# Alpha's signs made later, and other filler products at the start, in a banded attention with a PReLU feed-forward

## The chip, the cores and the metric

One core of a Trainium2 chip runs the program. TensorE (PE; PEld is its weight load) multiplies, VectorE (DVE), ScalarE (ACT) and GpSimd (POOL) do the elementwise work, and DMA queues on SyncE (SP) and ScalarE move data. The metric is the device time of one execution in microseconds: the median of 3 runs of the kernel before is 830.37 us (830.01 to 830.52).

## The reference

Attention in a causal window of 64 positions over 8 batches of 576 positions and 8 heads of 64, and behind it a feed-forward layer with a leaky rectifier whose slope alpha differs by hidden unit:

```python
scores = scale * np.matmul(q, k.transpose(0, 1, 3, 2))
mask = (rel >= 0) & (rel < window)
scores = np.where(mask, scores, -1000000000.0)
...
x = attn_out.transpose(0, 2, 1, 3).reshape(4608, 512)
h = x @ w_in                                       # 512 -> 2048
g = np.maximum(h, 0.0) + alpha * np.minimum(h, 0.0)
out = g @ w_out                                    # 2048 -> 512
```

The weights arrive as 64-bit floats and are taken apart on the chip into a high and a low 32-bit part.

## The kernel before

The 4608 tokens are 36 tiles of 128, in nine groups of four. For a tile, TensorE makes scores (`score`, L594), VectorE masks them and takes the row's maximum (L636), ScalarE takes the exponential (L642), VectorE the reciprocal of its sum (`recip`, L668 and L669), GpSimd scales (`scale`, L673), TensorE turns the result over (`turn`, L690), ScalarE or VectorE copies it from PSUM (`put`, L695 and L697), TensorE multiplies with the values (`value`, L733), and two more steps split that into a high and a low part (`x_high` L742, `x_low` L745). A hidden block of 128 units and its share of the output make a cell: `hidden` (L1204), the rectifier (L840, L847), its two parts (L853, L857), and the output products (L874). In the first 100 us the same engines also convert the 32 weight blocks (`weights`): `expo` (L436, L438), `shift` (L443, L446), `tail` (L451), `join` (L455), `total` (L459) and the two parts (L474, L478).

The rectifier needs, per hidden unit, the sign of 1 - alpha and alpha times that sign (`s_sb`, `sa_sb`); the sign bit (`flip_sb`) is also put into each block of `w_out` by its `shift`. `signs` makes all three from alpha, which was loaded, and turned by TensorE into a PSUM bank (`alpha_t`).

Every piece is a step with planned engine times; a planner puts the steps in order with a table of due times (`DUE`, `BEGIN`), and each engine's queue is written out in that order and worked off strictly in turn. Behind the plan, `fill` looks at TensorE's planned gaps up to 28 us and fills them with products that nobody reads (`plan.idle`, L391): a 128x128 block of zeros times itself, in 32-bit floats, into a spare PSUM bank. A product in 32-bit floats runs as two passes on the chip, each with its weight load. At the far end `quarter` (L1167, L1165, L1171) sums and stores the last four quarters of the output; a wanted time sets their order.

Of the kernel before, what the change touches and what calls it, by code (L numbers as in the profile page):

```python
# [18 lines left out]
PE, DVE, ACT, POOL, SP = "PE", "DVE", "ACT", "POOL", "SP"  # L19
# [6 lines left out]
WARM = 28.0  # L26
# [105 lines left out]
class Plan:  # L132
# [5 lines left out]
    def step(self, engines, emit, after=(), behind=(), take=(), give=(), want=math.inf, moved=0.0, span=0.0,  # L138
             port=False):

        s = Step(engines, emit, after, list(behind), list(take), list(give), want, moved, span, port)
        for a in s.after + s.behind:
            a.before.append(s)
        s.group = self.group
        self.steps.append(s)
        return s
# [110 lines left out]
    def fill(self, done):  # L260

        some, t = [], 1.3
        for s in sorted((s for s in done if s.engine == PE), key=lambda s: s.start):
            while t + 0.4 < min(s.start, WARM):
                hold = 0.22 if t > 6.0 else 0.3
                some.append(Step({PE: (hold, hold)}, self.idle, (), (), (), (), math.inf, 0.0, 0.0, False))
                some[-1].start, some[-1].end, some[-1].engine = t, t + hold, PE
                t += hold
            t = max(t, s.start + s.engines[PE][0])
        return some  # L270
# [28 lines left out]
def banded_attention_then_prelu_ffn(  # L299
# [11 lines left out]
    nc = tc.nc  # L311
    P = 128
    D = 64
    W = WINDOW
# [40 lines left out]
    sa_sb = const.tile([P, NF], F32, name="sa_sb")  # L355
# [30 lines left out]
    plan = Plan(stock)  # L386
    plan.stock["o"].append((WARM + 1.0, 3))
    spare = ps.tile([P, P], F32, tag="b3", name="spare")
    nought = xs_of["l", 1][:, 0, (NBLK - 1) * P:].bitcast(F32)
    nc.vector.memset(nought, 0.0)  # L390
    plan.idle = lambda _: nc.tensor.matmul(spare, nought, nought, start=True, stop=True)  # L391
    step = plan.step

    def turned_in(x):
# [14 lines left out]
    def room(b, shape, dtype, name):  # L409
        return sb.tile(shape, dtype, tag=str(b.at), name=name)  # L410
# [5 lines left out]
    def weights(c):  # L416
        plan.group = "w", c, 0
        f, odd = divmod(c, 2)
        d = cv[c]
        last = 2 * NF - 1 - c  # L420
        raw = Buffer("raw", 2, [None, "new", "v", "kk"][max(0, 3 - last)])
        val, low = (Buffer(kind, 1, "os" if last < 2 else None) for kind in ("val", "low"))
        two = Buffer("o" if c < 4 else "bank", 1)

        def fetch(_):
            t = room(raw, [P, 2 * E] if odd else [P, NP, 2 * P], I32, f"raw_{c}")
            nc.sync.dma_start(t, w_out[f * P:(f + 1) * P, :] if odd else
                              w_in[:, 2 * f * P:2 * (f + 1) * P].rearrange("(c p) f -> p c f", p=P))
            t = t if odd else t.rearrange("p a b -> p (a b)")
            t = t.rearrange("p (n t) -> p n t", t=2)  # L430
            d["low"], d["high"] = t[:, :, 0].bitcast(U32), t[:, :, 1]

        def expo(e):
            d["two"] = t = bank(two, [P, E], I32, f"two_{c}")
            if e == ACT:
                nc.scalar.activation(t.bitcast(F32), d["high"].bitcast(F32), AF.Copy, scale=2.0**-112)  # L436
            else:
                nc.vector.tensor_scalar(out=t.bitcast(F32), in0=d["high"].bitcast(F32), scalar1=2.0**-112,  # L438
                                        scalar2=None, op0=ALU.mult)

        def shift(_):
            if odd:
                nc.vector.tensor_scalar(out=d["two"], in0=d["two"], scalar1=3, scalar2=flip_sb[:, f:f + 1],  # L443
                                        op0=ALU.logical_shift_left, op1=ALU.bitwise_xor)
            else:
                nc.vector.tensor_scalar(out=d["two"], in0=d["two"], scalar1=3, scalar2=None,  # L446
                                        op0=ALU.logical_shift_left)

        def tail(_):
            d["tail"] = room(low, [P, E], I32, f"low_{c}")  # L450
            nc.scalar.activation(d["tail"], d["low"], AF.Copy, scale=2.0**-29)  # L451

        def join(_):
            d["val"] = room(val, [P, E], I32, f"val_{c}")
            nc.vector.scalar_tensor_tensor(out=d["val"], in0=d["high"], scalar=-2**31, in1=d["two"],  # L455
                                           op0=ALU.bitwise_and, op1=ALU.bitwise_xor)

        def total(_):
            nc.gpsimd.tensor_tensor(out=d["val"], in0=d["val"], in1=d["tail"], op=ALU.add)  # L459

        name = "wout" if odd else "win"

        def late(part):
            return [Buffer("late " + z, 1) for n, f0, z in LATE if (n, f0) == (name + part, f)]

        def begin(part):
            for n, f0, z in LATE:
                if (n, f0) == (name + part, f):
                    f1 = min([x for m, x, _ in LATE if m == n and x > f0], default=NF)
                    parts_of[n][f0] = sb.tile([P, f1 - f0, E], F32R, tag=z, name=f"{n}_{f0}")  # L470

        def high(_):
            begin("_h")
            nc.scalar.copy(weight(name + "_h", f), d["val"].bitcast(F32))  # L474

        def rest(e):
            begin("_l")
            (nc.gpsimd if e == POOL else nc.vector).tensor_tensor(  # L478
                out=weight(name + "_l", f), in0=d["val"].bitcast(F32), in1=weight(name + "_h", f).bitcast(F32),
                op=ALU.subtract)  # L480

        s0 = step({SP: (0.4, 0.4)}, fetch, take=[raw], moved=1.5 if odd else 1.65, span=1.75 if odd else 2.3)
        s1 = step({ACT: (0.55, 0.63), DVE: (0.6, 0.69)}, expo, [s0], take=[two])
        s2 = step({DVE: (0.66, 0.75) if odd else (0.6, 0.69)}, shift, [s1] + [alphas] * odd)
        s3 = step({ACT: (0.56, 0.66)}, tail, [s0], take=[low], give=[raw])
        s4 = step({DVE: (0.6, 0.68)}, join, [s2], take=[val], give=[raw, two])
        s5 = step({POOL: (1.22, 1.28)}, total, [s3, s4], give=[low])
        prior = cv[c - 2]["done"] if c >= 2 else [None, None]
        s6 = step({ACT: (0.51, 0.61)}, high, [s5], prior[:1] if prior[0] else [], take=late("_h"))
        s7 = step({POOL: (1.22, 1.28), DVE: (0.59, 0.68)}, rest, [s6], prior[1:] if prior[0] else [],  # L490
                  take=late("_l"), give=[val], port=True)
        d["done"] = [s6, s7]
# [340 lines left out]
    def behind(ts, f, d, done, hb, want_o, cols, coarse=True):  # L833
# [2 lines left out]
        gb, ghb, glb = Buffer("g", 1), Buffer("gh", 1), Buffer("gl", 1)  # L836

        def slopes(_):
            d["g"] = room(gb, [P, NBLK * P], F32, f"g_{ts[0]}_{f}")[:, :nt]
            nc.scalar.activation(d["g"], d["h"][:, :nt], AF.Copy, scale=sa_sb[:, f:f + 1])  # L840


        start = ts[0] < NBLK
# [33 lines left out]
        hold = {2: (1.46, 0.37, 0.40, 0.31, 0.69), 4: (2.72, 0.57, 0.667, 0.53, 1.24)}[n]  # L877
        lat = {2: (1.55, 0.475, 0.485, 0.405, 0.74), 4: (2.87, 0.69, 0.75, 0.62, 1.28)}[n]
        if f == 0:
            for t in ts:  # L880
# [5 lines left out]
                  give=[hb if start else gb])  # L886
# [3 lines left out]
        for todo in todos:  # L890
# [5 lines left out]
                      give=[ghb] + [glb] * lows, want=want_o)  # L896
# [5 lines left out]
        if f == NF - 1:  # L902
# [3 lines left out]
            for i, t in enumerate(ts):  # L906
                for x in parts(t):
                    sbuf, os = Buffer("g" if t == NT - 1 else "gh" if t == NT - 2 else "os", 1), {}
# [11 lines left out]
                    def store(e, t=t, x=x, os=os):  # L920
# [6 lines left out]
                             give=[ob[t]], want=want_o + 3 + i)  # L927
                    step({ACT: (0.4, 0.4)} if x.start else {SP: (0.4, 0.4)}, store, [c],
                         give=old if apart else [sbuf], moved=0.8 / m)
# [4 lines left out]
    entries_o, kept_o, slots, acc, mid = {}, {}, {}, {}, {}  # L934
# [49 lines left out]
    def behind_last(ts, f, d, done, hb, want_o, cols):  # L984
# [5 lines left out]
        lh, rh = slice(0, 2 * P), slice(2 * P, 4 * P)  # L990
# [127 lines left out]
        a1 = step(half, lambda _: vec(slots[i][:, rh], slots[i][:, rh], d["g"][:, rh], ALU.add), [s2], port=True)  # L1118
# [63 lines left out]

        last, u4_of = lambda: acc["P1"], lambda: u["u4"]
        quarter("os", 1, lh, lambda: acc["P7"], lambda: u["u2"], [p4, u2, u4], want_o + 3.0)
        quarter("os", 1, rh, u4_of, lambda: mid["P7"], [u4], want_o + 3.2)
        quarter("gh", 0, rh, lambda: acc["P3"], lambda: u["u4"], [p3, u4], want_o + 3.5)
        quarter("gl", 0, lh, last, None, [p2], want_o + 4.0)

# [228 lines left out]
    al, ab = {}, Buffer("o", 1)  # L1417
# [2 lines left out]
        al["t"] = bank(ab, [P, NF], F32, "alpha_t")  # L1420
        nc.tensor.transpose(al["t"], alpha_sb, ident[:NF, :NF])

    def signs(_):
        a = al["t"]
        nc.vector.tensor_scalar(out=s_sb, in0=a, scalar1=1.0, scalar2=-2.0, op0=ALU.is_gt, op1=ALU.mult)
        nc.vector.tensor_scalar_add(s_sb, s_sb, 1.0)
        nc.vector.tensor_scalar(out=flip_sb, in0=s_sb.bitcast(I32), scalar1=-2**31, scalar2=None, op0=ALU.bitwise_and)
        nc.vector.tensor_tensor(out=sa_sb, in0=s_sb, in1=a, op=ALU.mult)

    a0 = step({ACT: (0.64, 0.64)}, load_alpha, moved=0.1)  # L1430
    a1 = step({PE: (0.2, 0.4)}, turn_alpha, [a0], take=[ab])
    alphas = step({DVE: (0.8, 0.8)}, signs, [a1], give=[ab], want=20.0)

    plan.group = "z", 0, 0
    new = Buffer("new", 1, "pt")
# [123 lines left out]
```

## Time and profile before

| | us |
|---|---|
| median of 3 runs | 830.37 |
| the profiled execution | 831.18 |
| its span, from the first to the last instruction | 829.3 |
| PE busy in it | 819.8 (99%) |
| DVE busy | 596.6 (72%) |
| ACT busy | 486.3 (59%) |
| POOL busy | 426.2 (51%) |

The busy share of PE counts the filler products too, and is an average over a start in which other engines set the pace and a long stretch in which PE does. The granted clock is 1.00 over the span.

### The profile page before, as it was taken

What the parts mean: (1) busy time and instruction counts of PE and PEld (TensorE: products, weight loads), DVE (VectorE), ACT (ScalarE), POOL (GpSimd) and SP (SyncE); (2) the same over time, 40 slices, a digit from 0 to 9 for tenths busy, and PEclk for the clock granted to TensorE, in tenths of its full rate; (3) what the DMA queues carried; (4) which work ended last, traced back from release to release, by engine and by line L of the source; (5) the groups of instructions that cost most, each with busy time, mean ns of one, the idle gap of its engine ahead of it and who ended that gap; (6) DMA issues with size and microseconds to landing.
All of it is one profiled execution on the core that took longest, in us unless ns stands there. A gap on an engine that the chain in (4) does not pass through costs nothing.

```text
span 829.3 us, 21484 instructions
## 1 busy us (share of the span) xinstructions
PE 819.8 (99%) x7943; PEld 748.3 (90%) x7943; DVE 596.6 (72%) x1675; ACT 486.3 (59%) x1297; POOL 426.2 (51%) x424
## 2 busy tenths in 40 slices
PE   9999999999999999999999999999999999999997
PEld 8888888888999999999999999999999999998997
DVE  6999979997666573888496678658787639525665
ACT  6999986567464634655454646465646446434542
POOL 4888776896433333646365435544454533222462
PEclk9999999999999999999999999999999999999999
DMA  9587756484766566776677675768676765467765
GB/s 312 188 269 212 211 183 202 171 264 142 241 180 202 154 183 211 230 197 193 225 193 240 191 252 153 247 183 244 197 242 180 217 202 150 109 215 224 242 219 165
DMA packets 128679, 170.75 MB, mean 206 GB/s; under 512 B 9776, under 2 KB 82496, under 8 KB 128576
## 3 DMA queue, kind: packets, MB, share of 16 engines
q1 hardware_dynamic: 127408, 168.34, 66.8%
q8 instruction: 63, 1.03, 0.5%
q10 hardware_dynamic: 1168, 1.06, 0.4%
q14 instruction: 40, 0.33, 0.1%
HBM read 141.04 MB, written 28.31 MB: 204 GB/s over the span
## 4 chain that ended last, share of the span: by engine, by line
PE 92%; ACT 3%; DVE 2%; DMA 1%; POOL 1%; issue 1%; SPq 0%; DVEq 0%; ACTq 0%; POOLq 0%
PE o L874 38%; PE h L1336 31%; PE h L1204 8%; PE acc_P L1045 4%; PE av L733 4%; PE s L612 3%; PE s L594 1%; PE spare L391 1%; DMA win_h<-kept 1%; PE t L690 1%; DVE val L455 1%; ACT low L451 0%; POOL val L459 0%; ACT two L436 0%; DMA out<-os 0%
## 5 line engine op out<-in xcount | busy, mean ns | idle before, releaser
L857 POOL TENSOR_TENSOR gl<-g,gh 128x512 fp32r<-128x512 f32 x112 | 144.3, 1296 | 207.5 <-ACT gh L853 121.3
L874 PE MATMUL o<-wout_h,gh 128*128 128x512 f32 x512 | 196.9, 385 | 0.0
L874 PE MATMUL o<-wout_l,gh 128*128 128x512 f32 x512 | 194.2, 379 | 0.0
L840 ACT ACTIVATE g<-h,sa_sb 128x512 f32<-128x512 f32 (+1 forms) x132 | 89.2, 676 | 127.8 <-DVE h L1363 113.9
L874 PE MATMUL o<-wout_h,gl 128*128 128x512 f32 x512 | 136.0, 379 | 0.0
L713 DVE STREAM_TRANSPOSE pt<-w 32x256 f32<-32x256 f32 x312 | 128.5, 426 | 4.7
L847 DVE SCALAR_TENSOR_TENSOR g<-h,s_sb,g 128x512 f32<-128x512 f32 x112 | 83.9, 749 | 33.9 <-ACT g L840 32.4
L874 PEld LDWEIGHTS o<-wout_h,gh 128*128 128x128 f32 x512 | 97.1, 190 | 12.2 <-issue 0.5
L874 PEld LDWEIGHTS o<-wout_h,gl 128*128 128x128 f32 x512 | 95.8, 189 | 13.2 <-POOL gl L857 0.2
L874 PEld LDWEIGHTS o<-wout_l,gh 128*128 128x128 f32 x512 | 97.2, 190 | 9.6 <-DVE wout_l L478 0.3
L853 ACT CAST gh<-g 128x512 fp32r<-128x512 f32 x112 | 69.3, 620 | 49.4 <-DVE g L847 48.4
L1363 DVE TENSOR_TENSOR h<-h,w 128x256 f32<-128x256 f32 x56 | 24.2, 433 | 100.2 <-PE h L1336 98.3
L652 ACT ACTIVATE w<-w,nm 128x96 f32<-128x96 f32 x208 | 76.1, 373 | 13.4 <-DVE nm L646 13.3
L673 POOL TENSOR_TENSOR w<-w,rc 128x768 f32<-128x768 f32 (+2 forms) x44 | 59.0, 1341 | 46.3 <-DVE rc L669 35.6
L1373 ACT COPY u<-h 128x256 f32<-128x256 f32 x112 | 41.7, 373 | 53.8 <-PE h L1336 53.6
L1336 PE MATMUL h<-xh,win_l 128*128 128x256 f32 x336 | 64.9, 275 | 0.0
L1336 PE MATMUL h<-xh,win_h 128*128 128x256 f32 x336 | 63.5, 277 | 0.0
L1336 PEld LDWEIGHTS h<-xh,win_h 128*128 128x128 f32 x336 | 55.0, 190 | 6.9 <-DVE h L1363 0.3
L1336 PE MATMUL h<-win_h,win_l 128*128 128x256 f32 x336 | 59.8, 281 | 0.0
L1363 DVE TENSOR_TENSOR h<-h,u 128x256 f32<-128x256 f32 x112 | 47.5, 427 | 12.4 <-PE h L1336 8.0
L1336 PEld LDWEIGHTS h<-xh,win_l 128*128 128x128 f32 x336 | 51.8, 192 | 0.5
L1336 PEld LDWEIGHTS h<-win_h,win_l 128*128 128x128 f32 x336 | 50.0, 191 | 0.9
(205 smaller groups left out, 1855.2 us busy)
## 6 DMA issues: line engine op xcount, KB each, us to landing
win_h<-kept SPq DMA_DIRECT2D x112, 256.0 KB, 2.8
win_l<-kept SPq DMA_DIRECT2D x112, 256.0 KB, 3.0
v<-vN SPq DMA_DIRECT2D x72, 256.0 KB, 4.6
stream<-kept SPq DMA_DIRECT2D x56, 256.0 KB, 2.9
k<-kT SPq DMA_DIRECT2D x35, 384.0 KB, 4.1
q<-qT SPq DMA_DIRECT2D x34, 256.0 KB, 4.4
raw<-w_in SPq DMA_DIRECT2D x16, 512.0 KB, 4.3
raw<-w_out SPq DMA_DIRECT2D x16, 512.0 KB, 4.1
```

Source lines behind the costliest of these rows:

```text
L652: nc.scalar.activation(w, w, AF.Exp, scale=-1.0, bias=d["nm"][:, g:g + 1], accum_out=d["sm"][:, g:g + 1])
L673: nc.gpsimd.tensor_tensor(out=w, in0=w, in1=d["rc"][:, g].unsqueeze(2).broadcast_to(list(w.shape)), op=ALU.mult)
L713: nc.vector.transpose(dst[:, :, i * SUB:(i + 1) * SUB], d["w"][r, :, :, k * SUB:(k + 1) * SUB].rearrange("p e h k -> p (e h) k"))
L840: nc.scalar.activation(d["g"], d["h"][:, :nt], AF.Copy, scale=sa_sb[:, f:f + 1])
L847: nc.vector.scalar_tensor_tensor(out=g, in0=d["h"][:, :nt], scalar=s_sb[:, f:f + 1], in1=d["g"], op0=ALU.mult, op1=ALU.max)
L853: nc.scalar.copy(d["gh"], d["g"])
L857: (nc.vector if start else nc.gpsimd).tensor_tensor(out=d["gl"], in0=d["g"], in1=d["gh"].bitcast(F32), op=ALU.subtract)
L874: nc.tensor.matmul(po[t], gt[:, cols[i] * P:(cols[i] + 1) * P], turned_in(weight(wt, f)), start=(f == 0 and k == 0), stop=(f == NF - 1 and ...
L1204: nc.tensor.matmul(ph[:, :nt], weight(wt, f)[:, c * P:(c + 1) * P], turned_in(tokens_of(xt, xs)[:, c]), start=(k == 0), stop=(k == 3 * NP ...
L1336: nc.tensor.matmul(out, a[:, c * P:(c + 1) * P], turned_in(b[c]), start=start and i == c == 0, stop=i == 2 and c == 1, skip_group_check=True)
L1363: nc.vector.tensor_tensor(out=out, in0=a, in1=b, op=ALU.add)
L1373: nc.scalar.copy(d["u"][i], d[x])
```

## The change

The time at which alpha's signs are made moves: the step that ran `signs` behind alpha's turn now only copies alpha from PSUM to `sa_sb` (`take_alpha`), and the four instructions of `signs`, now reading that copy, are sent from inside the first `shift` of a `w_out` block. `fill` has other bounds: before 11 us of planned time it leaves gaps of up to 0.3 us open, from there to 24 us up to 1.1 us, then 0.5 us (it was 0.4 us throughout); and up to 6 us it puts in pairs of products with 48 moving columns (`plan.cold`) with a planned 0.4 us a pair, in place of one of 128 with 0.3 us. One wanted time at the end is 0.5 us later.

```diff
-            while t + 0.4 < min(s.start, WARM):
-                hold = 0.22 if t > 6.0 else 0.3
-                some.append(Step({PE: (hold, hold)}, self.idle, (), (), (), (), math.inf, 0.0, 0.0, False))
+            while t + (0.3 if t < 11.0 else 1.1 if t < 24.0 else 0.5) < min(s.start, WARM):
+                hold = 0.22 if t > 6.0 else 0.4
+                some.append(Step({PE: (hold, hold)}, self.idle if t > 6.0 else self.cold, (), (), (), (), math.inf, 0.0, 0.0, False))
...
+    def cold(_):
+        for _ in range(2):
+            nc.tensor.matmul(spare[:, :W * 3 // 4], nought, nought[:, :W * 3 // 4], start=True, stop=True)
...
         def shift(_):
+            if odd and not al.get("done"):
+                al["done"] = True
+                signs()
             if odd:
...
-        quarter("os", 1, rh, u4_of, lambda: mid["P7"], [u4], want_o + 3.2)
+        quarter("os", 1, rh, u4_of, lambda: mid["P7"], [u4], want_o + 3.7)
...
-    def signs(_):
-        a = al["t"]
+    def take_alpha(_):
+        nc.vector.tensor_copy(sa_sb, al["t"])
+
+    def signs():
+        a = sa_sb
         nc.vector.tensor_scalar(out=s_sb, in0=a, scalar1=1.0, scalar2=-2.0, op0=ALU.is_gt, op1=ALU.mult)
         nc.vector.tensor_scalar_add(s_sb, s_sb, 1.0)
         nc.vector.tensor_scalar(out=flip_sb, in0=s_sb.bitcast(I32), scalar1=-2**31, scalar2=None, op0=ALU.bitwise_and)
         nc.vector.tensor_tensor(out=sa_sb, in0=s_sb, in1=a, op=ALU.mult)
...
-    alphas = step({DVE: (0.8, 0.8)}, signs, [a1], give=[ab], want=20.0)
+    alphas = step({DVE: (0.8, 0.8)}, take_alpha, [a1], give=[ab], want=20.0)
```

TensorE's queue from its first instruction, before (spare is the bank of the filler products, s are scores, t the turned weights of the softmax, x9 nine products in a row):

```order
L391 MATMUL spare<-xl_101 128x128 x9
L594 MATMUL s_0_0_151<-k_127,q_125 64x128
...
L391 MATMUL spare<-xl_101 128x128 x6
L594 MATMUL s_0_0_192<-k_135,q_133 64x128
...
L1421 MATMUL alpha_t<-ident,alpha_sb 128x16
L391 MATMUL spare<-xl_101 128x128 x6
L690 MATMUL t_0_244<-ident,w_103 128x128 x4
L391 MATMUL spare<-xl_101 128x128 x4
L690 MATMUL t_1_263<-ident,w_103 128x128 x4
```

The same place now:

```order
L395 MATMUL spare<-xl_101 128x48 x14
L603 MATMUL s_0_0_156<-k_127,q_125 64x128
...
L391 MATMUL spare<-xl_101 128x128 x7
L603 MATMUL s_0_0_198<-k_137,q_135 64x128
...
L391 MATMUL spare<-xl_101 128x128
L1430 MATMUL alpha_t<-ident,alpha_sb 128x16
L391 MATMUL spare<-xl_101 128x128 x7
L699 MATMUL t_0_249<-ident,w_103 128x128 x4
L699 MATMUL t_1_268<-ident,w_103 128x128 x4
```

Nine wide filler products ahead of the first scores became fourteen narrow ones, six between the first and the second tile's scores became seven, and the four between the two turns are gone. Behind this place, up to the second cell's start, the filler counts 5, 5, 1, 4 and 3 became 2, 1, 0, 1 and 2. The real work keeps its order.

VectorE's queue where alpha's signs were made, before (rc is the softmax reciprocal, w the masked scores):

```order
L669 RECIPROCAL rc_90<-rc_90 128x4
L1425 TENSOR_SCALAR s_sb<-alpha_t 128x16
L1426 TENSOR_SCALAR s_sb<-s_sb 128x16
L1427 TENSOR_SCALAR flip_sb<-s_sb 128x16
L1428 TENSOR_TENSOR sa_sb<-s_sb,alpha_t 128x16
L636 ISA w_104,nm_91<-s_0_0_192,masks 128x2x64
```

And the place further down the same queue, now, where they are made (xl is the low part of a tile's attention, two the block of `w_out` in hand):

```order
L754 TENSOR_TENSOR xl_99<-av_310,xh_98 128x4x128
L1438 TENSOR_SCALAR s_sb<-sa_sb 128x16
L1439 TENSOR_SCALAR s_sb<-s_sb 128x16
L1440 TENSOR_SCALAR flip_sb<-s_sb 128x16
L1441 TENSOR_TENSOR sa_sb<-s_sb,sa_sb 128x16
L452 TENSOR_SCALAR two_300<-two_300,flip_sb 128x512
```

At the first place one copy, `L1434 COPY sa_sb<-alpha_t 128x16`, stands in for the four; at the second the four stand between `x_low` and `shift`, whose own neighbours are unchanged. At the end of the program, the stores of the quarter that GpSimd sums and of the one that VectorE sums change places on SyncE's and ScalarE's queues, and nothing else moves there.

## Rows read from the trace of the kernel before

**Rows 1.** The page, section 4: shares of the chain that ended last, by engine.

```profile
PE 92%; ACT 3%; DVE 2%; DMA 1%; POOL 1%; issue 1%; SPq 0%; DVEq 0%; ACTq 0%; POOLq 0%
```

**Rows 2.** Stretches (us): busy time and instructions of PE, PEld, DVE, ACT, POOL; granted clock; DMA.

```profile
40.00:100.00 60.00, 59.83 (x431) 51.31 (x431) 55.56 (x130) 56.20 (x123) 48.96 (x40) 1.00 0.74 225
200.00:800.00 600.00, 598.83 (x5905) 554.71 (x5904) 405.85 (x1138) 319.13 (x859) 265.20 (x276) 1.00 0.68 203
```

**Rows 3.** The chain that ended last, 0 to 40 us: start, us, what.

```profile
1.12 4.21 PE spare L391 x18
5.33 1.65 PE s L594 x32
6.98 1.54 PE spare L391 x12
8.52 1.10 PE s L594 x32
```

**Rows 4.** DMA issues: tile, queue, count, KB each, median us from issue to landing.

```profile
q<-qT ACTq DMA_DIRECT2D x2, 128.0 KB, 3.3
q<-qT ACTq DMA_DIRECT2D x1, 256.0 KB, 6.0
```

**Rows 5.** Timeline, the first queries' loads: start, us, queue, what.

```profile
0.82 1.38 ACTq L536 DMA_DIRECT2D q<-qT  x3
```

**Rows 6.** By line: count, min/median/max ns, first and last start in us.

```profile
L391 PE MATMUL spare<-xl x86: 275/275/579, 1.1 to 25.7; 128*128 128x128 f32 x86
L594 PEldq EVENT_SEMAPHORE  x15: 51/51/51, 3.8 to 138.4; - x15
```

**Rows 7.** Timeline around alpha's signs: start, us, engine, what, idle before and its releaser.

```profile
10.32 0.14 DVE L1425 TENSOR_SCALAR s_sb<-alpha_t 128x16 f32<-128x16 f32 x1
10.56 1.04 POOL L673 TENSOR_TENSOR w<-w,rc 128x512 f32<-128x512 f32 x1 [6.99 <-ACT w L642]
10.71 0.92 DVE L1427 TENSOR_SCALAR flip_sb<-s_sb 128x16 int32<-128x16 int32 x1
11.55 0.16 DVE L1428 TENSOR_TENSOR sa_sb<-s_sb,alpha_t 128x16 f32<-128x16 f32 x1
11.85 0.63 PE L690 MATMUL t<-ident,w 128*128 128x128 f32 x4 [0.60 <-DVE sa_sb L1428]
11.95 0.40 ACT L642 ACTIVATE w<-w,nm 128x128 f32<-128x128 f32 x1 [1.08 <-DVE nm L636]
```

**Rows 8.** Timeline around the first shift that uses the signs.

```profile
18.20 1.28 POOL L459 TENSOR_TENSOR val<-val,low 128x512 int32<-128x512 int32 x1 [0.28 <-DVE rc L668]
19.12 0.75 DVE L443 TENSOR_SCALAR two<-two,flip_sb 128x512 int32<-128x512 int32 x1
19.44 1.04 POOL L673 TENSOR_TENSOR w<-w,rc 128x512 f32<-128x512 f32 x1
19.71 0.59 ACT L695 COPY pt<-t 128x512 f32<-128x512 f32 x1 [0.19 <-PE t L690]
20.87 0.29 DVE L636 CUSTOM_DVE_ANT_0 w<-s,masks 128x128 f32<-128x128 f32 x1 [0.20 <-PE s L594]
20.89 1.29 POOL L478 TENSOR_TENSOR win_l<-val,win_h 128x512 fp32r<-128x512 f32 x1 [0.41 <-ACT win_h L474]
```

**Rows 9.** L668 beside GpSimd: one of its runs, and its ns by line.

```profile
23.65 0.80 DVE L668 TENSOR_SCALAR rc<-sm 128x4 f32<-128x4 f32 x1
L668 DVE TENSOR_SCALAR rc<-sm x44: 145/168/796, 10.0 to 694.4; 128x8 f32<-128x8 f32 x28, 128x4 f32<-128x4 f32 x16
```

**Rows 10.** Timeline: a VectorE sum with both inputs in SBUF beside GpSimd.

```profile
805.61 1.38 DVE L1011 TENSOR_TENSOR kept_g_l<-kept_g_l 128x256 f32<-128x256 f32 x1
```

**Rows 11.** Timeline of the last sums, and the last stores by line.

```profile
822.97 1.53 POOL L1167 TENSOR_TENSOR quarter<-u,pt 128x512 f32<-128x512 f32 x1 [10.14 <-DVE u L1148]
823.54 0.75 DVE L1167 TENSOR_TENSOR quarter<-acc_P,u 128x512 f32<-128x512 f32 x1
L1171 ACTq DMA_DIRECT2D out<-quarter x4: 577/632/767, 823.6 to 826.1; - x4
```

More of the change, by code (lines that the diff above doesn't have):

```diff
@@ L391, in banded_attention_then_prelu_ffn @@
     plan.idle = lambda _: nc.tensor.matmul(spare, nought, nought, start=True, stop=True)
+    def cold(_):
+        for _ in range(2):
+            nc.tensor.matmul(spare[:, :W * 3 // 4], nought, nought[:, :W * 3 // 4], start=True, stop=True)
+    plan.cold = cold
     step = plan.step
@@ L838, in slopes @@
         def slopes(_):
+            assert al["done"]
             d["g"] = room(gb, [P, NBLK * P], F32, f"g_{ts[0]}_{f}")[:, :nt]
```

## The prediction

> **What bounds the kernel now.** I read the chain that ended last first: TensorE has 92% of it [rows 1]. Where it has it, the stretches tell: between 40 and 100 us TensorE stands still for 0.17 us, between 200 and 800 us for 1.17 us [rows 2]. From about 40 us on the product stream is the bound, so whatever the change gains or loses at the start reaches the end whole, and it can reach it nowhere else but in the last stores. Within the start, the chain runs through 4.21 us of filler products, the first scores (1.65 us), 1.54 us of filler, the second tile's scores (1.10 us) [rows 3], then into VectorE. There two waits point at the edit: TensorE's first turn waited 0.60 us for alpha's last sign instruction, and ScalarE's softmax stood idle 1.08 us until VectorE, done with the signs, masked on [rows 7]. So the start is a relay between VectorE, ScalarE and GpSimd, and each term has to be followed to the engine that is late next.
>
> **Fillers ahead of the first scores.** Nine products of two passes are 18 in 4.21 us, about 0.21 us a pass, and the longest record is twice the shortest (579 against 275 ns [rows 6]), so TensorE starts at the lower of its two levels. The loads of the first queries were issued at 0.82 us and from there on about every 0.46 us (1.38 us for three) and take 3.3 us [rows 4, 5], so they are there at 4.1 and 4.6 us, and TensorE's queue already passed a wait of the scores at 3.8 us [rows 6]. The scores start at 5.33 [rows 3]: 1.2 us of that is filler. Now there are 28 passes with 48 of 128 moving columns but the same 128-column weights. No row shows such a pass. From below it is 48/128 of 0.21 us, 0.08, in all 2.2 us; from above it is 0.21 us, if the weights take that long, in all 5.9 us. The nearest row of that weight shape at the short duration is the 1.54 us of 12 filler passes behind the scores, 0.13 us each [rows 3]; I take 0.13 for the cost of one weight load with a short product, 28 of them 3.6 us, so scores at about 4.8: 0.5 us earlier. The ends give 1.1 us earlier (the loads then decide) and 1.7 us later. For a 128-column weight load the Trainium skill has a formula (TensorE: Matmul & The Clock Gate, LDWEIGHTS) that comes to 107 ns; 28 of these are 3.0 us, 0.6 us less than mine.
>
> **Fillers behind them.** Seven for six is 2 passes, 0.26 us late. The third query load (issue near 1.74, 6.0 us [rows 4, 5]) lands at 7.7 us, so the second scores, now at 8.52 [rows 3], can gain 0.7 at most; 0.5 less 0.26 leaves about 0.3 us.
>
> **Signs taken out.** The four hold VectorE from 10.32 to 11.71, 1.39 us [rows 7]; the copy costs what the first of them did, 0.14. That frees 1.25 us. But the turn behind also needs GpSimd's scaling, 10.56 to 11.60 [rows 7]; with the 0.3 us above it ends at 11.3, against the turn's 11.85. So 0.55 us is what the turn and VectorE's copy of its result gain; the rest becomes a wait of VectorE for the turn. ScalarE's gap of 1.08 us closes, but its next work hangs on masks that stand behind that copy, so it too keeps only about 0.55.
>
> **Signs put back.** They now stand at 19.12, in front of the shift [rows 8], and all they cost is on VectorE's queue, with the shift, the last mask of a tile, a weight join and the next tile's masks behind them, and ScalarE's softmax waiting for those. Their own time is about 0.15 each, 0.6 us. But the flip, the same shape, took 0.92 us beside a GpSimd operation that began 0.15 us before it and ended with it [rows 7], and the reciprocal's first half took 796 ns at most against 168 as a rule [rows 9]. At 19.12 GpSimd is busy from 18.20 to 20.48 and again from 20.89 [rows 8]. From below the four cost 0.6; from above each of the first two waits for the end of a GpSimd operation: 19.48, 20.48, then the other two, done at about 20.85, 1.7 us. I take what they cost before, 1.4 us, between the two. VectorE is then 0.85 us late.
>
> **What is late next.** VectorE idled 0.20 us at 20.87 for the next scores [rows 8], which come earlier now: of five fillers ahead of the last turn in front of them four are gone, 8 passes of 0.13 us, 1.0 us (ScalarE's copy waited only 0.19 us for that turn [rows 8], so by itself that is worth no more). Late by 0.65, VectorE comes to the reciprocal at 23.65, which stood 0.80 us for GpSimd instead of 0.17 [rows 9]: up to 0.63 us are absorbed there, on the chain's path. ScalarE, whose softmax got its masks late, hides nothing. I put 0.3 us on the path out of the start; with the bounds of the fillers and of the signs it lies from 1.0 us gained to 2.3 us lost.
>
> **Last stores.** VectorE's sum, done at 824.29, is now stored before GpSimd's, done at 824.50 [rows 11], so the second pair of stores goes out 0.2 us earlier, and the last issue at 826.1 can follow: its data are VectorE's last copy. 0.2 us gained, or nothing.
>
> **Sum.** +0.3 - 0.2 = +0.1 us on the profiled 831.18, 831.3. That execution is 0.8 us above the median of 830.37, so on the runs' scale 830.5, and I say 830.4: no change. What a measurement of this kernel can tell from no change is about 0.2%, 1.7 us.
>
> **Rivals.** First, the gains carry: fillers at their lower end, 1.1 us, of which 0.7 us reaches the second scores (the load decides), all 1.25 us of the signs with it, and the signs put back beside an idle GpSimd at 0.6 us, within VectorE's 0.20 us wait and the reciprocal's 0.63: -0.7 - 1.25 - 0.2 = -2.2, 828.2 us. For it: both waits of [rows 7] go. Against: GpSimd's scaling ends the same wait 0.1 us before the signs do. Second, the other side, with one place: the weight load of a narrow pass costs as much as the wide pass did. 28 at 0.21 us put the first scores at 7.0, 1.7 us late, and the second (the first take 1.10 or 1.65 us, the fillers 1.8) at 9.9 to 10.5, 1.4 to 2.0 late. It decides from 0.25 us of delay on, what GpSimd's scaling had in hand before the turn. At 1.6 us the turn is 1.4 late; with the signs' 1.4, less the 0.8 absorbed and the 0.2 of the stores, +1.8: 832.2 us. For it: the weights keep all 128 columns. Against: the filler passes at 0.13 us have them too. Third, TensorE stays at its lower level (1.2 GHz, by the doubled durations) through the second scores, since it was fed less before: these take 1.65 instead of 1.10, and fourteen passes 0.21 instead of 0.13, 1.7 us late, less the 0.3 gained; the turn is then 1.15 late, and by the same sum +1.5: 831.9 us, more if it lasts into the turns. For it: the short durations came only after 4 us of wide products. Against: the scores are full work.
>
> Fourth, the signs meet three GpSimd operations. A VectorE sum of two SBUF tiles took 1.38 us beside GpSimd [rows 10]; the fourth sign instruction read PSUM and now reads SBUF twice. Done third at about 20.7, it loses to GpSimd's 1.29 us of 20.89 [rows 8] if ScalarE, no longer 0.19 us late, lets that start 0.2 us sooner: 3.0 us for the signs instead of 1.4, 832.0. The Trainium skill has this as a rule (SBUF — State Buffer, Who interferes with whom): a VectorE instruction with two SBUF inputs, or a tensor_scalar in its two-port mode, waits for the whole of a GpSimd instruction that reads SBUF and started first. The rows above agree with both halves.
>
> **How the numbers follow.** No change 0.58, the gains carry 0.17, dear weights 0.13, lower level 0.06, three operations 0.06. The forecast's own spread seldom crosses 1.7 us; of the three slow cases, all priced at 1.5 to 1.8, two thirds lie beyond it, since their prices are the smaller ends. So faster 0.17, within 0.2% 0.64, slower 0.19. The range takes in most of the gain and the losses at their price: 828.8 to 832.3; the likeliest case alone spans 829.6 to 831.3.
>
> **What would show it.** Right: the first scores start near 4.8 and the second near 8.2; the turn no longer waits for `sa_sb`; VectorE waits for the turn instead; the four instructions in front of the shift take over 1 us together, two of them as long as a GpSimd operation; the first cell's hidden products start within 0.5 us of where they did. Wrong: first scores later than 5.3 (dear weights), scores of the second tile at 1.65 us (lower level), or signs at 0.6 us in all with those products over 1 us earlier (the gains carry).

## The result, and the profile after

The changed kernel takes 838.05 us (median of 6 runs, 837.22 to 839.04), the kernel before beside it 830.81: a ratio of 1.0085, 95% interval 1.0072 to 1.0099, 7.1 us slower. The forecast was 830.4, and 832.3 the end of its range. The profiled execution took 838.87 us with a span of 837.0 us, against 829.3 before: 7.7 us.

TensorE still has nearly all of the chain that ended last (page, section 4; before in [rows 1]):

```profile
PE 91%; DVE 2%; DMA 2%; ACT 2%; POOL 1%; issue 1%; SPq 0%; DVEq 0%; ACTq 0%
```

So the loss is sought in the start, as the gain was. The chain after (start, us, what); L395 are the narrow products, L391 the wide ones, L603 the scores, L699 the turn, L1438 to L1441 the four sign instructions, L1214 the hidden products:

```profile
1.13 6.21 PE spare L395 x28
7.33 1.92 PE s L603 x32
9.25 2.51 PE spare L391 x14
11.76 1.03 PE s L603 x32
...
13.37 1.76 PE spare L391 x14
15.13 0.45 PE t L699 x4
...
22.19 0.32 DVE s_sb L1438
...
22.54 0.97 DVE s_sb L1439
23.53 0.18 DVE flip_sb L1440
23.71 1.15 DVE sa_sb L1441
24.86 0.67 DVE two L452
...
28.55 2.93 PE h L1214 x12
...
44.65 1.60 PE h L1214 x12
```

Held against [rows 3] and [rows 7], the delay grows in three places. The first scores start at 7.33 instead of 5.33 and the second at 11.76 instead of 8.52: 2.0 and 3.2 us late. The same fourteen filler passes took 2.51 us and, 4 us later, 1.76: the trace's first record of TensorE's granted clock begins at 10.78 us of the span, in before at 6.58. Ahead of its first record a trace has no clock, and the stretches print 1.00 there, so the 1.00 over the span of before says nothing of its first 6.58 us. The passes tell the level: from start to start they are 0.21 us apart until that record begins and 0.11 us behind it, in both kernels. The signs in front of the shift, from 22.19 to 24.86, take 2.7 us. And the first cell's hidden products start at 28.55 instead of 23.29 and take 2.93 us. Their first four in the timeline of before:

```profile
23.29 0.69 PE L1204 MATMUL h<-xh,win_h 128*128 128x256 f32 x4
```

The stretches of after show why (columns as in [rows 2]; the column behind the five engines is the granted clock, 0.50 being the lower level):

```profile
24.00:26.00 2.00, 0.18 (x3) 0.15 (x2) 2.00 (x5) 0.24 (x1) 0.83 (x1) 1.00 0.12 45
26.00:28.00 2.00, 0.73 (x6) 0.53 (x5) 1.97 (x14) 2.00 (x10) 1.27 (x1) 0.96 0.33 33
28.00:32.00 4.00, 3.45 (x16) 3.45 (x17) 3.88 (x13) 3.11 (x11) 3.29 (x3) 0.50 0.49 180
40.00:100.00 60.00, 58.97 (x410) 50.58 (x410) 54.87 (x119) 54.84 (x116) 49.05 (x41) 1.00 0.75 231
```

From 24 to 28 us TensorE has 0.9 us of work while VectorE is busy throughout; then its clock is at 0.50 until 34.7 us; before's trace has no such fall between its first rise and its last products. The last chain row above answers to one of before, shown here:

```profile
38.38 1.60 PE h L1204 x12
```

By it 6.3 of the 7.7 us are there at 44.65. Another 1.0 us is lost between 47 and 82 us, where a load of the weights stands in the chain for 5.2 us. That is not the change's: between 40 and 100 us TensorE stands still for 1.03 us here against 0.17 in before [rows 2], but for 1.13 and 1.33 us in two kernels below that can't be told from before in time, the one with half the narrow products and the one with the signs on GpSimd. The profiled execution of before is one without that wait. The stretch in these two, in that order:

```profile
40.00:100.00 60.00, 58.87 (x426) 50.18 (x425) 54.26 (x126) 54.85 (x118) 48.52 (x40) 1.00 0.70 222
40.00:100.00 60.00, 58.67 (x425) 50.02 (x424) 54.11 (x126) 54.76 (x118) 48.50 (x40) 1.00 0.72 222
```

### The profile page after: what moved, and what is told of

The parts are those of the page before. It is cut to its first block, busy times and chain, and to the rows that moved or that the text cites. A ratio compares the mean times of both kernels' runs of the same rounds, so it can differ in the third digit from the quotient of the medians.

```text
span 837.0 us, 21453 instructions
## 1 busy us (share of the span) xinstructions
PE 823.6 (98%) x7927; PEld 751.4 (90%) x7927; DVE 597.7 (71%) x1676; ACT 485.3 (58%) x1297; POOL 425.8 (51%) x424
## 3 DMA queue, kind: packets, MB, share of 16 engines
q8 instruction: 63, 1.03, 0.5%
## 4 chain that ended last, share of the span: by engine, by line
PE 91%; DVE 2%; DMA 2%; ACT 2%; POOL 1%; issue 1%; SPq 0%; DVEq 0%; ACTq 0%
PE o L884 38%; PE h L1346 31%; PE h L1214 8%; PE av L742 4%; PE acc_P L1055 4%; PE s L621 3%; PE s L603 1%; PE spare L395 1%; DMA win_h<-kept_o 1%; PE spare L391 1%; DMA raw<-w_in 1%; PE t L699 1%; DMA win_h<-kept 1%; POOL val L468 1%; DVE w L645 0%
```

## The experiments

All ratios are to the kernel before on the same chip, with 95% intervals; 0.001 is 0.83 us. The change has four parts: the signs (copy early, four instructions in front of the shift), the narrow products ahead of the first scores, the fewer fillers from 11 us on, and the order of the last stores. A fifth, small one, the bound from 6 to 11 us, which adds a few filler products, is in the last two rows of the table only.

| what of the change is in | us | ratio |
|---|---|---|
| signs | 831.63 | 1.0005 (0.9996 to 1.0014) |
| narrow products | 834.84 | 1.0044 (1.0030 to 1.0057) |
| fewer fillers | 831.06 | 1.0002 (0.9994 to 1.0011) |
| last stores | 830.67 | 0.9995 (0.9983 to 1.0008) |
| signs, narrow products | 835.35 | 1.0045 (1.0031 to 1.0059) |
| signs, fewer fillers | 833.96 | 1.0032 (1.0019 to 1.0046) |
| narrow products, fewer fillers | 834.55 | 1.0037 (1.0024 to 1.0049) |
| all four | 838.05 | 1.0085 (1.0072 to 1.0099) |

### One part at a time

Signs alone: the changed kernel with before's fill and last stores.

```
-            while t + (0.3 if t < 11.0 else 1.1 if t < 24.0 else 0.5) < min(s.start, WARM):
-                hold = 0.22 if t > 6.0 else 0.4
+            while t + 0.4 < min(s.start, WARM):
+                hold = 0.22 if t > 6.0 else 0.3
...
```

> The kernel before with the move of the signs alone (copy early, four sign instructions in front of the shift); fillers and last stores as before. Theory A (three prices added: dear narrow products, signs slowed by GpSimd, TensorE short of work from 24 to 34 us): the four signs take 1.4 to 2.7 us at their new place, the early copy frees about 0.5 us, so about +1 us, 831.5 to 832.5, and the granted clock stays at 2.4 GHz. Rival B (the signs carry nearly all of the 7.7 us, the rest follows from them): 835 or more. Rival C (everything comes from the fillers and the clock): within 0.5 us of before.

Measured 1.0005, 0.4 us: as a time that is Rival C's figure and less than half of Theory A's. Of A's terms, the four take 1.6 us, the clock stays up, and the early copy brings the turn 0.1 us forward, not 0.5. In its timeline (start, us, engine, line, what) the copy only lets VectorE run into GpSimd's scaling, for which the reciprocal's first half, 0.16 us in before, now waits:

```profile
10.64 1.04 POOL L676 TENSOR_TENSOR w<-w,rc 128x512 f32<-128x512 f32 x1 [7.08 <-DVE sa_sb L1428]
10.66 1.04 DVE L671 TENSOR_SCALAR rc<-sm 128x4 f32<-128x4 f32 x1
```

And the four end with two short ones, because GpSimd stood still for 0.38 us:

```profile
19.25 1.04 POOL L676 TENSOR_TENSOR w<-w,rc 128x512 f32<-128x512 f32 x1
20.68 1.28 POOL L481 TENSOR_TENSOR win_l<-val,win_h 128x512 fp32r<-128x512 f32 x1 [0.38 <-ACT win_h L477]
...
19.36 0.96 DVE L1433 TENSOR_SCALAR s_sb<-s_sb 128x16 f32<-128x16 f32 x1
20.36 0.17 DVE L1434 TENSOR_SCALAR flip_sb<-s_sb 128x16 int32<-128x16 int32 x1
20.44 0.17 DVE L1435 TENSOR_TENSOR sa_sb<-s_sb,sa_sb 128x16 f32<-128x16 f32 x1
```

The second waits for GpSimd's scaling; the flip and the product slip into the gap. Rival B is out. Rival C, that nothing comes from the signs, is answered below, where they meet the fewer fillers.

Narrow products alone: before with the new products ahead of the first scores.

```
+    def cold(_):
+        for _ in range(2):
+            nc.tensor.matmul(spare[:, :W * 3 // 4], nought, nought[:, :W * 3 // 4], start=True, stop=True)
...
-            while t + 0.4 < min(s.start, WARM):
-                hold = 0.22 if t > 6.0 else 0.3
+            while t + (0.3 if t < 6.0 else 0.4) < min(s.start, WARM):
+                hold = 0.22 if t > 6.0 else 0.4
...
```

> The kernel before with the narrow filler products ahead of the first scores alone (28 passes with 48 moving columns in place of 18 with 128); later fillers, signs and last stores as before. Theory A: first scores at 7.3 instead of 5.3 us, the clock rises only at about 10.8 us of the span, second scores at about 11.5; 3 us later at the first turn, less 0.8 us that later waits absorb: +2 to +2.5, about 833. Rival B (signs): the start's delay is absorbed, within 1 us of before. Rival C (fillers and clock): +4 or more.

Measured 1.0044 (1.0030 to 1.0057), 3.7 us: half of the whole loss, and more than Theory A's 2 to 2.5, nearer C's 4 or more. Its chain:

```profile
1.12 6.21 PE spare L395 x28
7.33 1.92 PE s L600 x32
9.25 2.21 PE spare L391 x12
11.45 1.10 PE s L600 x32
```

The first clock record begins at 10.61 us. The first turn is 2.9 us late, and so is the row that stands at 38.38 in before: nothing of the 0.8 us that A took off was absorbed.

Fewer fillers alone: `0.4` becomes `(0.4 if t < 11.0 else 1.1 if t < 24.0 else 0.5)`, the rest as before.

> The kernel before with the fewer fillers from 11 us on alone (a gap under 1.1 us, later 0.5, gets none). Theory A: the scores in front of the fifth filler group come about 1 us earlier, of which the wait for masks keeps 0.2; in the stretch from 24 to 28 us, where before has work for TensorE, the clock does not fall: between -0.5 and +0.5 us. Rival C (missing fillers let the clock fall by themselves): the granted clock is 0.5 somewhere between 18 and 36 us and the time is 2 us or more longer.

Measured 1.0002, Theory A's no change. But in the profiled execution the clock was at 0.5 from 14.6 to 18.0 us, behind 4 us in which TensorE had 2.45 us of work; A had not expected that:

```profile
14.60:18.00 3.40, 3.40 (x45) 2.85 (x46) 2.53 (x17) 2.82 (x12) 1.04 (x1) 0.50 1.10 386
```

Its mean clock of 0.998 was reached in no other of the 11 runs, so the part alone seldom lets the clock fall.

Last stores alone: `want_o + 3.2` becomes `want_o + 3.7`.

> The kernel before with the order of the last stores alone. In the profile of the changed kernel the end comes 4.3 us after TensorE's last product instead of 4.5. Theory A: -0.2 us, not to be told from no change. Rival: the store that now goes first holds the queue for the others, +0.3 or more.

Measured 0.9995: as a time it can't be told from nothing. The profiles are sharper: in that of the changed kernel the end comes 4.31 us after TensorE's last product, in that of before 4.50, and all five with the new order have 4.31 to 4.33, all eleven with the old one 4.49 to 4.51.

### Two parts at a time

Signs and narrow products: the changed kernel with before's later fillers and last stores (the condition as for the narrow products alone).

> The kernel before with the signs moved and the narrow filler products ahead of the first scores; later fillers and last stores as before. Measured so far, against before: signs alone +0.3 us, narrow products alone +3.5, fewer later fillers alone -0.2, all of the change +7.2; so 3.6 us come from edits meeting. Theory A (late signs leave TensorE without work and, the later fillers being gone, the clock falls a second time): this one keeps the later fillers, so the two add up, +3.8, 835.1, and the granted clock does not fall after its first rise. Rival F (the late start pushes the signs into the third GpSimd operation, that is where the 3.6 us lie): +6 or more, the sa_sb instruction over 1 us, with the clock up.

Measured 1.0045: the sum of the two, 1.0049, lies in the interval, as Theory A has it. The product `sa_sb` took 168 ns, and there is no second fall in its trace. Rival F is out: the late start by itself does not bring the third GpSimd operation.

Signs and fewer fillers (conditions as in the parts alone, wide products ahead of the first scores):

> The kernel before with the signs moved and fewer fillers from 11 us on; the wide products ahead of the first scores and the last stores as before. Theory A: the pair that makes the second fall of the clock: it is at 0.5 for some us between 22 and 35 us, the first cell's hidden products take 2.9 instead of 1.6 us, +2.5 to +3.5, about 834. Rival G (the second fall needs the late start of the narrow products): +0.1, 831.4, the clock up throughout or down only where the kernel with fewer later fillers alone had it.

Measured 1.0032, 2.7 us, where the two parts have 0.4 and 0.2. Rival G is out, and with it the Rival C of the signs alone: without their move the fewer fillers cost 0.2 us. Two things are new in its trace. The timeline:

```profile
18.21 1.04 POOL L676 TENSOR_TENSOR w<-w,rc 128x512 f32<-128x512 f32 x1
19.36 1.26 POOL L481 TENSOR_TENSOR win_l<-val,win_h 128x512 fp32r<-128x512 f32 x1
...
19.32 0.17 DVE L1434 TENSOR_SCALAR flip_sb<-s_sb 128x16 int32<-128x16 int32 x1
19.41 1.25 DVE L1435 TENSOR_TENSOR sa_sb<-s_sb,sa_sb 128x16 f32<-128x16 f32 x1
```

and its stretches (columns as above):

```profile
20.00:24.00 4.00, 0.85 (x6) 0.69 (x6) 3.96 (x18) 2.44 (x11) 2.04 (x3) 1.00 0.30 61
24.00:28.00 4.00, 3.66 (x18) 3.66 (x19) 3.79 (x13) 2.91 (x11) 3.35 (x4) 0.57 0.44 168
```

With the fillers gone, the turn in front of ScalarE's copy comes sooner, ScalarE no longer waits 0.19 us for it, and GpSimd starts its third operation without the gap. The product of two SBUF tiles then takes 1.25 us instead of 0.17. TensorE has 0.85 us of work in the 4 us before the first cell, and its clock falls.

Both changes of the fillers, signs and stores as before:

> The kernel before with both changes of the fillers, narrow ahead of the first scores and fewer from 11 us on; signs and last stores as before. Theory A: the two add up, +3.3, 834.6, since without the late signs TensorE has work from 24 to 28 us. Rival H (the fillers make all of the loss by themselves, the signs matter not): +6.5 or more, 838.

Measured 1.0037, Theory A's sum; no second fall in its trace. Rival H is out.

### What the narrow products do

The changed kernel with 128 moving columns in each of the 28 passes:

```
-            nc.tensor.matmul(spare[:, :W * 3 // 4], nought, nought[:, :W * 3 // 4], start=True, stop=True)
+            nc.tensor.matmul(spare, nought, nought, start=True, stop=True)
```

> The changed kernel, but the 28 passes ahead of the first scores have 128 moving columns instead of 48, with the same weights. If the weight load sets a pass at the lower level, the first scores still start at 7.3 us (0.21 to 0.22 us a pass). Theory A: if the narrow products also keep the clock low, it now rises at about 6.6 us as before, so the first scores take about 1.1 us instead of 1.92 and the 14 passes behind them 1.8 instead of 2.5: 1.5 us earlier at the second scores, and 836.5 to 837.5 in all. Rival D (the clock rises late because of the scores' own pauses, not the narrow products): the rise stays near 10.8 us and the time at 838. Rival E (columns set the pass): first scores later than 9 us.

Measured 834.95 (1.0043 to before): 3 us less than the changed kernel, more than the 0.5 to 1.5 that A gave. There is more work in each pass, and the passes are sooner done:

```profile
1.12 4.86 PE spare L395 x28
5.98 1.03 PE s L603 x32
7.01 1.76 PE spare L391 x14
8.77 1.09 PE s L603 x32
```

The first clock record begins at 4.23 us. So the 28 passes took 4.86 us instead of 6.21, which A (7.3 us for the scores) had wrong as well; D and E are out. What is left to before is the pair of signs and fewer fillers (1.0032) and ten more passes; its trace has the second fall too, from 24.7 to 31.5 us.

Half the narrow products, in before (14 passes: `range(1)` in `cold`):

> The kernel before, but ahead of the first scores 14 narrow passes (48 moving columns, 128-column weights), half as many as in the changed kernel; the rest as before. So far: 28 narrow passes took 0.22 us each and the clock rose only at 10.6 to 12.8 us of the span in four kernels, 3.3 to 5.4 us after the first scores began; with wide products it rose at 4.1 to 6.6 us. Theory A (a narrow pass costs as much as a wide one, and narrow products do not raise the clock): scores start at the landing of their load, near 4.6 us, take 1.8 to 2.0 us, and the clock rises only at 7.5 to 10 us; the second scores start at 8.7 to 9.2, +0.3 to +0.8 us, 831.3. Rival J (the late rise came from the late scores alone): the clock rises at 4 to 6.6 us and the second scores start at about 8.2, -0.3 to 0 us.

Measured 1.0004 (0.9995 to 1.0013), and the clock record begins at 7.86 us, behind the first scores, as Theory A has it:

```profile
1.13 3.22 PE spare L395 x14
4.35 1.92 PE s L600 x32
6.27 2.31 PE spare L391 x12
8.58 1.10 PE s L600 x32
```

The scores began one microsecond sooner than in before and, at the lower level until they were done, gave it back. Rival J is out.

The narrow product turned round, 28 passes in before:

```
-            nc.tensor.matmul(spare[:, :W * 3 // 4], nought, nought[:, :W * 3 // 4], start=True, stop=True)
+            nc.tensor.matmul(spare[:W * 3 // 4], nought[:, :W * 3 // 4], nought, start=True, stop=True)
```

> The kernel before, but ahead of the first scores 28 passes with 48-column weights and 128 moving columns: the shape of the narrow products turned round; the rest as before. Theory A (the weight load sets the 0.22 us of a narrow pass): a pass falls to about 0.11 us, the first scores start at their load, near 4.6 us, and the time is within 0.5 us of before. Rival K (a pass of this type has a floor of 0.21 us at the lower level, whatever its weights): first scores at 6 to 7.3 us. On the clock: if the moving columns are what raises it, it rises at 4 to 6.6 us as with the wide products; if it is the filled part of the array, it rises after 10 us and the time is near 834.5.

Measured 1.0014 (1.0005 to 1.0023), 1.2 us:

```profile
1.12 5.62 PE spare L395 x28
6.74 1.03 PE s L600 x32
7.78 1.53 PE spare L391 x12
9.31 1.10 PE s L600 x32
```

The clock record begins at 5.99 us; up to there, at some 0.21 us a pass, 23 of the 28 are done. Theory A's name for the price was wrong: a pass of 48-column weights takes as long as one of 128, from start to start 0.21 us ahead of the clock record and 0.11 behind it. Rival K holds: at the lower level such a pass takes 0.21 to 0.23 us with 128 by 128, with 48 moving columns and with 48-column weights. The Trainium skill (TensorE: Matmul & The Clock Gate, LDWEIGHTS) lets the load time grow with the weights' columns; the records of the loads show that (203 ns with 48 columns against 333 with 128, medians), a pass of these products does not. And the clock rose as with the wide products: in ten profiles with these it rose at 4.1 to 6.6 us, in four with 28 narrow ones at 10.6 to 12.8, always behind the first scores. Of the 3.7 us of the narrow products, 1.2 are thus the number of passes, and 2.5 the clock that stays low (by the changed kernel with wide products, 3.1).

### What the signs and the fewer fillers do together

The product behind the shift instead of in front of it, in the kernel of that pair:

```
-        nc.vector.tensor_tensor(out=sa_sb, in0=s_sb, in1=a, op=ALU.mult)
...
+                if "sa" not in al:
+                    al["sa"] = True
+                    nc.vector.tensor_tensor(out=sa_sb, in0=s_sb, in1=sa_sb, op=ALU.mult)
```

> The kernel with the signs moved and fewer fillers from 11 us on (833.96, +2.7 us; wide products ahead of the first scores, last stores as before), but the fourth sign instruction, the product of two SBUF tiles, is issued behind the shift instead of in front of it. Theory M (GpSimd's third operation is the price): the shift starts 1.1 us earlier, the product meets at most the rest of that operation, 0.4 us; the first cell comes about 0.8 us earlier and TensorE's idle time with it, no fall of the clock: +0.5 to +1.2 us, 831.5 to 832.3. Theory N (the fall of the clock is the price and comes from the missing fillers alone): the clock still falls between 20 and 28 us, +2 us or more.

Measured 1.0024 (1.0014 to 1.0033), outside what M gave, and 0.7 us under the pair, which the intervals don't separate. The trace shows M's steps (shift at once, the product's wait cut to the rest of GpSimd's operation):

```profile
20.29 0.76 DVE L446 TENSOR_SCALAR two<-two,flip_sb 128x512 int32<-128x512 int32 x1
20.96 0.45 DVE L450 TENSOR_TENSOR sa_sb<-s_sb,sa_sb 128x16 f32<-128x16 f32 x1
```

What M missed is the clock. Each run lists its mean granted clock; a fall like those above takes 0.002 or more off it, though the kernel before reads 0.998 too in four of 93 runs, and never less. Six of the 11 runs have 0.999 or 1.000 and a median of 832.15 us, M's figure; five have 0.994 to 0.998 and a median of 833.68. By these medians the fall is worth some 1.5 us here, and comes in about half of the executions. The groups are small and overlap: the slowest run of all, 834.32, is one of the six.

Fillers back in front of the first cell only: `0.5` and `1.1 if t < 24.0` become `0.4` and `1.1 if t < 18.0`.

> The same pair of edits, but ahead of the first cell five filler products (10 passes, about 1.3 us) stand again where before has them, and only there and behind. Theory M: the fourth sign instruction still takes 1.25 us; the fillers run while TensorE waits for VectorE, so they delay nothing; if they keep the clock up, about 1 us of the 2.7 comes back, 833.0; if 10 passes are too few and the clock falls all the same, 833.9. Theory N: the clock stays up and at least 2 us come back, 832 or less.

Measured 1.0024 (1.0014 to 1.0034), 833.31 us, and a mean clock of 0.999 or 1.000 in all nine runs, while the pair has 0.994 to 0.998 in seven of eight. The product still meets GpSimd:

```profile
20.36 1.26 DVE L1435 TENSOR_TENSOR sa_sb<-s_sb,sa_sb 128x16 f32<-128x16 f32 x1
```

So with the clock held up the pair costs 2.0 us, 0.4 of it the signs alone, and by subtraction some 1.6 the third GpSimd operation. The profiles make that 1.0: the row of 38.38 stands at 39.00 with the signs alone and at 39.97 here. That the fillers hold the clock up, the nine runs against seven of eight show; what the fall costs, 0.7 us between 1.0024 and 1.0032, the intervals don't separate. That is Theory M's first branch, with 833.31 for its 833.0; N is out. In the changed kernel all six runs have 0.996 to 0.998, and the lowest are not the slowest: the two at 0.998 took 837.74 and 838.18 us, the three at 0.996 837.22 to 838.87.

### The signs elsewhere

On GpSimd, behind its second softmax scaling (last stores in the new order):

```
-            if odd and not al.get("done"):
-                al["done"] = True
-                signs()
+                al["n"] = al.get("n", 0) + 1
+                if al["n"] == 2:
+                    al["done"] = True
+                    signs()
...
-        nc.vector.tensor_scalar(out=flip_sb, in0=s_sb.bitcast(I32), scalar1=-2**31, scalar2=None, op0=ALU.bitwise_and)
+        nc.gpsimd.tensor_scalar(out=flip_sb, in0=a, scalar1=1.0, scalar2=-2.0**31, op0=ALU.is_gt, op1=ALU.mult)
...
```

> The kernel before with the early copy and the four sign instructions on GpSimd, right behind its second softmax scaling, where GpSimd stood still for 1.7 us; the flip is made from alpha directly; last stores in the changed kernel's order, fillers as before. Theory A (the signs cost because they stand on VectorE's queue beside GpSimd): with fillers of before the signs moved alone cost 0.4 us, of which 1.2 us were lost in front of the shift; that goes, the earlier turn stays: 0.5 to 1.0 us faster, 829.6 to 830.3, first cell's hidden products at about 23.0 us. Rival L (four small GpSimd instructions take over 0.4 us each and hold up the third scaling): +0.5 us or more.

Measured 830.62, 0.9992 (0.9983 to 1.0001): Theory A's size, with the 0.2 us of the stores in it, and not safely told from no change. The four fit into GpSimd's idle time; the next scaling waits for VectorE as before:

```profile
13.12 0.28 POOL L1435 TENSOR_SCALAR s_sb<-sa_sb 128x16 f32<-128x16 f32 x1
13.49 0.27 POOL L1436 TENSOR_SCALAR s_sb<-s_sb 128x16 f32<-128x16 f32 x1
13.72 0.28 POOL L1437 TENSOR_SCALAR flip_sb<-sa_sb 128x16 int32<-128x16 f32 x1
14.09 0.22 POOL L1438 TENSOR_TENSOR sa_sb<-s_sb,sa_sb 128x16 f32<-128x16 f32 x1
14.84 1.04 POOL L673 TENSOR_TENSOR w<-w,rc 128x512 f32<-128x512 f32 x1 [0.52 <-DVE rc L669]
```

The same with fewer fillers from 11 us on:

> As the kernel with the signs on GpSimd, and with fewer fillers from 11 us on, the wide products ahead of the first scores kept. With the signs in front of the shift this pair of edits cost 2.7 us. Theory A (it is the signs' time on VectorE's queue that leaves TensorE idle and lets the clock fall): no fall between 20 and 30 us, -1.0 to 0 us, 829.8 to 830.8. Rival G (fewer fillers let the clock fall wherever the signs stand): the granted clock is 0.5 for some us in the start and the time is 832 or more.

Measured 830.62, 0.9990 (0.9981 to 1.0000), a mean clock of 0.999 or 1.000 in all 11 runs: in these runs fewer fillers do no harm where the signs don't hold VectorE up, and rival G is out again. With the one above this is the best version: by the ratios 7.9 us under the changed kernel, and 0.8 us under the kernel before, with an interval that ends at no change.

## Why the prediction was wrong

That the start decides, and that what it loses reaches the end, held: 6.3 of the 7.7 us are there at 44.65 us. The forecast failed in the steps of the start.

**Fillers ahead of the first scores.** The step that failed is "I take 0.13 for the cost of one weight load with a short product". That duration came from passes behind the rise of the clock [rows 3], and I carried it into a stretch in front of it. The measured 0.22 us is the upper bound, 0.21. Rival two, dear weights, put the scores at 7.0; they came at 7.33. Its cause is another: weights of 48 columns cost a pass as much. Rival three, the lower level, came in the same run, in part: the first scores took 1.92 us and the fourteen passes 2.51, but the second scores, which it put at 1.65, took 1.03, behind the rise. I gave the two separate chances and never priced both; its doubt, "the scores are full work", missed that the full work only begins at 7.33. Their delays, 1.7 us each, together 3.4, are near the 3.2 measured at the second scores (2.0 and 1.2). Their prices, 1.8 and 1.5, can't be added: each already has the signs' 1.4 in it, and takes off 0.8 us for later waits, of which the narrow products alone show nothing.

**Fillers behind them.** Seven for six was counted at 0.26 us. At the lower level the passes are no longer 0.13, and the second scores came 3.2 us late, not 0.3 early. That their load sets a limit was right, but not where: in the profile with the signs alone it lands at 8.40 us, not 7.7, and the scores start at 8.45, so there was 0.1 us to gain and not 0.7. It lands at 8.79 with the fewer fillers alone.

**Signs taken out.** Right in that GpSimd's scaling decides: with the signs alone the turn starts at 11.73 instead of 11.85. But what VectorE has freed does not become a wait for the turn: 0.87 us of the 1.25 go to the reciprocal, which now waits for that scaling (1.04 us instead of 0.17).

**Signs put back.** Alone, right: 19.02 to 20.61 in their chain, 1.6 us against 1.4 taken, and 0.4 us in the end. In the change it is 2.7. The step that failed is the worth of ScalarE's wait for the turn, "by itself that is worth no more" than 0.19 us. Those 0.19 us are half of the 0.38 us gap in GpSimd through which the flip and the product slipped. Rival four said so, with 3.0 us for the signs, and got 0.06. Its rule in the Trainium skill (SBUF — State Buffer, Who interferes with whom), that a VectorE instruction with two SBUF inputs waits for a GpSimd instruction that reads SBUF and started first, agrees: 0.17 us beside an idle GpSimd, 1.25 beside a busy one.

**What is late next.** The absorption held for the signs alone: the shift starts 1.45 us late, the row of 38.38 only 0.62. The fewer fillers were only counted as time given back. No term had what they were for: VectorE being late, TensorE had nothing to do for some 3 us, and the clock fell. The sentence "more if it lasts into the turns" thought of the first rise alone.

**Last stores.** -0.2 us, as the profile shows (4.31 against 4.50), too small for the runs: right.

**Sum.** Narrow products 3.7, the pair of signs and fewer fillers 2.7 (0.4 signs, 1.0 to 1.6 the third GpSimd operation, the rest the fall): 6.4, within the 6.0 to 8.2 of the whole. How much of it is the fall stays open: no run takes it alone out of the changed kernel, where it lasts 6.8 us against 3.4 in the pair. Each loss stood in the prediction as a rival but the second fall; besides the price of a pass, the mistake was to let them exclude one another.

## What to carry to other kernels

Take a duration only from a stretch at the clock level in which the instruction will run, and treat "cheaper" filler as untested work: at the lower level three shapes of pass cost the same, and the one with few moving columns left the clock low. Where a stage is a relay between engines, a small wait of one can be what keeps two others apart; before removing it, lay the timelines over each other without it. Rivals that can happen in one run need a joint price.

## What was not expected of the hardware

- 28 passes with 128 moving columns were done in 4.86 us, 28 with 48 in 6.21: the clock rose at 4.23 us, among the former, and at 10.78, when the latter had ended at 7.33.
- When the clock rises differs between executions with the same start: 4.1 to 6.6 us in the nine profiles with the same 18 wide passes, by which the first scores started at 4.71 to 5.26 us, 0.5 us that no edit made. So does whether it falls: with the product behind the shift, the profile has no fall though TensorE had 1.46 us of work from 20 to 24 us.
- Four small sign instructions on GpSimd take 0.22 to 0.28 us each; on VectorE beside GpSimd they took 0.17 to 1.25.
